# Due times of the first loads in a planned attention and convolution kernel: values of batch 0 one pair later, shared keys of batch 1 cast as they land

## The chip, the cores and the metric

The kernel runs on one core of a Trainium2 chip. The metric is the device time of one execution in microseconds (us). The span of a profile is the time from the first to the last instruction of one profiled execution.

The engines are named as the profile names them: PE is TensorE's matmul (PEld its weight load), DVE is VectorE, ACT is ScalarE, POOL is GpSimd, SP is SyncE, which here only issues DMAs.

## The reference

The input is q, k and v of 8 batches, 12 heads, 448 positions and 64 features, all float32, with three weight arrays. Attention has a softmax whose denominator has one more term; its result goes through a gated long convolution:

```python
scores = scale * np.matmul(q, k.transpose(0, 1, 3, 2))
m = np.max(scores, axis=-1, keepdims=True)
e = np.exp(scores - m)
attn = e / (np.sum(e, axis=-1, keepdims=True) + np.exp(-m) + 1e-09)
attn_out = np.matmul(attn, v)
...
proj = x @ w_proj                      # x: attn_out with the heads side by side, 448 x 768
x1, x2, x3 = three thirds of proj
X2 = np.fft.rfft(x2, n=S, axis=1)
H = np.fft.rfft(filter_fft, n=S, axis=0)
x2_conv = np.fft.irfft(X2 * H, n=S, axis=1)
y = x1 * x2_conv * x3
out = y @ w_out
```

## The kernel before, in words

**Work.** Heads are taken in pairs, six to a batch, so there are 48 pairs, numbered g = 0 to 47 through all batches. For a pair, TensorE makes scores transposed (keys on partitions; L662, L664), ScalarE takes the exponential (L670, L675), TensorE multiplies by the values with a column of ones beside them (L707, L712), and VectorE divides (L725 to L727). Then the result is turned so that features lie on partitions (`xT`). When the six pairs of a batch are done, the dense part of the batch follows: VectorE folds `xT` into sums and differences (`xf`, L819 to L827), TensorE projects the folded input with the middle third of the weights (L850, the first matmul of the dense part of batch 0), goes to the spectrum and back with small tables (L877, L962), makes the two gates (L923) and the output projection (L1035). Attention of the next batch runs between the pieces of the dense part.

**Keys in four blocks.** A head has 448 keys: three blocks of 128 and a rest of 64. The rests of the two heads of a pair share one block. So each batch has, for all six pairs, one load of the rest keys and one of the rest values into the buffer `rests` (L333). There is one such buffer for all batches, and one buffer `ks`, into whose diagonal halves the rest keys are cast (L372). Transposes of every pair of a batch read `ks`, so the cast of batch 1 comes after the transposes of pair 5, the last of batch 0. The rest values are cast into `vr` (L377), which exists twice.

**The first two batches.** Batches 0 and 1 are loaded as float32 by SyncE in `staged` (k and v: L321, 192 KB for a pair each; q: L316, two loads of 112 KB; the very first q comes by ScalarE's queue). They land in four staging slots, so pair g needs slot g mod 4, freed by the casts of pair g-4. GpSimd casts them to bf16 (k L343, q L349, v L356); TensorE turns k and q (L384, L386, L390). Batches 2 to 7 are cast by GpSimd's DMAs while they load (`loaded`). GpSimd also issues the loads of the weights (L640: three loads of 1152 KB, the middle third first; L645 for the output weights) and of the filter (L555 to L559).

**What sets the order.** `Plan` writes out the order of every engine before the kernel runs. Each piece of work is a task with an engine, an estimated length, a due time ("want"), the tokens that it needs, those that it makes, and the buffers that it takes and gives. Whenever an engine is free in the plan, it gets the ready task with the smallest due time. The chip executes the resulting order of each engine as it stands; the waits are semaphores put in by the framework. Due times in `staged` come from `tau(g)`: 6 + 3.5 g for the pairs of batch 0, 31 + 5.5 (g - 6) for those of batch 1. Loads are due `early` before that: 8 for batch 0, 14 for batch 1, with 0.1 between the three loads of a pair (k, q, v for batch 0; v, q, k for batch 1). The casts are due at tau(g) - 5 for k and q, and for v at tau(g) + 1 in batch 0 and tau(g) - 4 in batch 1. Each task can name tokens made when it starts (`begun`), such as `iv` 5 for the value load of pair 5; the weights' issues use them as gates (`GATES`): the middle third (part 1) is due at 12 and is ready once the value load of pair 5, the shared loads and the k and q loads of pair 7 have been issued in the plan.

Of the kernel before, what the change touches and what calls it, by code (L numbers as in the profile page):

```python
# [20 lines left out]
SP = 112  # L21
# [20 lines left out]
class Plan:  # L42
# [15 lines left out]
        self.size = rings  # L58
        self.tasks = []

    def add(self, eng, cost, want, emit, need=(), make=(), take=(), give=(), dma=0.0, run=256, n=1, after=0.0, begun=()):
        self.tasks.append((want, len(self.tasks), eng, cost, emit, need, make, take, give, dma, after, run, n, begun))

    def run(self):
        left = {}
# [16 lines left out]
        clock = 0.0  # L82
        landed = []

        def done(t, end, by):
            for k in t[6]:
                made[k] -= 1
                when[k] = (max(end, when.get(k, (0.0, by))[0]), by)
                heapq.heappush(events, end + self.LAT[by])
                heapq.heappush(events, end)  # L90
            for tok in t[8]:
                left[tok] -= 1
                if left[tok] == 0:
                    gone[tok] = end + self.LAT[by]
                    heapq.heappush(events, gone[tok])

        def transfers(to):
            nonlocal clock
            while clock < to:
                heads = {e: q[0] for e, q in queues.items() if q and q[0][0] <= clock + 1e-9}  # L100
                soon = [q[0][0] for q in queues.values() if q and q[0][0] > clock + 1e-9]
                if not heads:
                    clock = min([to] + soon)
                    continue
                total = sum(h[2][11] for h in heads.values())
                step = min([h[1] * total / h[2][11] for h in heads.values()] + [x - clock for x in soon] + [to - clock])
                clock += step
                for e, h in heads.items():
                    h[1] -= step * h[2][11] / total
                    if h[1] <= 1e-9:  # L110
                        queues[e].pop(0)
                        if e == "SP":
                            landed.extend([clock + self.LANDING] * h[2][12])
                        done(h[2], clock + self.LANDING, "SP")

        def ready(t):
            e = t[2]
# [23 lines left out]
        while any(queue.values()):  # L141
            moved = False
            for e in queue:
# [18 lines left out]
                if t[9]:  # L162
                    q = queues["POOL" if e == "POOL" else "SP"]
# [20 lines left out]
def kernel(  # L184
# [13 lines left out]
    MAGIC = 12582912.0  # L198
    NSTAGED = 2
    SPIN = 40  # L200
    EARLY1 = 14.0
    SLOT1 = 5.5
    BASE2 = 77.0
# [4 lines left out]
    RE1 = 4.0  # L208
    FT = 8.0
    GATES = (  # L210
        (1, [("iv", 5), ("ir", 1), ("ik", 7), ("iq", 7)]), ("F", [("cv", 8)]), (0, [("cv", 9)]), (2, [("cv", 10)]),
        ("O", [("cv", 11)]),
    )
    STEP = 1.5
    FOLD0 = (28.5, 29.0, 29.5)
# [60 lines left out]
    add = plan.add  # L276
    ATT0, SLOT0 = 6.0, 3.5
# [3 lines left out]
    def tau(i, frac=0.0):  # L281

        if i < NHP:
            return ATT0 + SLOT0 * (i + frac)
        if i < 2 * NHP:
            return BASE + SLOT1 * (i + frac - NHP)
        return BASE2 + (i + frac - 2 * NHP) * PERIOD / NHP
# [12 lines left out]
    def staged(b):  # L300
# [3 lines left out]
        for hp in range(NHP):  # L304
            g = b * NHP + hp
            want = tau(g) - early
            parts = (("k", k, 0, 384), ("q", q, 768, 512), ("v", v, 384, 384))
            if b:
                parts = parts[::-1]
            for n, (name, x, at, size) in enumerate(parts):  # L310
                src = stage(g, at, size)

                def load(name=name, x=x, src=src, hp=hp, g=g):
                    if name == "q":
                        for u in range(2):
                            (nc.sync if g else nc.scalar).dma_start(  # L316
                                src[0:SP, 256 * u : 256 * u + 256].rearrange("p (j d) -> p j d", j=NST),
                                q[b, 2 * hp + u].rearrange("(j p) d -> p j d", j=NST),
                            )
                    else:  # L320
                        nc.sync.dma_start(  # L321
                            src.rearrange("p (u c) -> p u c", u=2), rows(x, b, hp)
                        )

                need = [("c" + name, g - 4)] if g >= 4 else []
                old = g - 2 * NHP
                first = name == "q" and g == 0
                add("ACT" if first else "SP", 1.04 if name == "q" else 0.52, -21.0 if first else want + 0.1 * n, load, need=need,
                    make=[("s" + name, g)], dma=0.97 if name == "q" else 0.64, run=256 if name == "q" else 768,
                    n=2 if name == "q" else 1, begun=[("i" + name, g)])  # L330
                if hp == 0 and name != "q":
                    add("SP", 0.5, want + (0.05 if name == "k" else SLOT0 + 0.05) if b == 0 else want - RE1 + 0.1 * n,
                        lambda name=name, x=x: nc.sync.dma_start(rests[:, "kv".index(name)], shared(x, b)),  # L333
                        need=[("cr" + name, b - 1)] if b else (), make=[("r" + name, b)],
                        dma=0.75, begun=[("ir", b)])

                on_pool = name == "k" or g > 0
                eng = nc.gpsimd if on_pool else nc.vector

                def cast(name=name, src=src, hp=hp, g=g, eng=eng):  # L340
                    if name == "k":
                        T[g]["kn"] = t = ld.tile([128, 3, 128], BF16, name="k0")
                        eng.tensor_copy(  # L343
                            t[:].rearrange("p j (u d) -> p u j d", u=2),
                            src.rearrange("p (u j d) -> p u j d", u=2, j=3),
                        )
                    elif name == "q":
                        T[g]["qn"] = t = ld.tile([SP, NST, 2, DH], BF16, name="q0")
                        eng.tensor_copy(  # L349
                            t[:].rearrange("p j u d -> p u j d"),  # L350
                            src[0:SP].rearrange("p (u j d) -> p u j d", u=2, j=NST),
                        )
                    else:
                        sv = src.rearrange("p (u j d) -> p u j d", u=2, j=3)
                        for u in range(2):
                            nc.gpsimd.tensor_copy(  # L356
                                vn[b % 2][:, hp, 4 * u : 4 * u + 3, 0:DH], sv[:, u]
                            )

                T.setdefault(g, {})  # L360
                if name == "v":
                    add("POOL", 0.72, tau(g) + (1.0 if b == 0 else -4.0), cast,
                        need=[("sv", g)] + ([("V", old, 1)] if b >= 2 else []), make=[("cv", g), ("v", g)])
                else:
                    add("POOL" if on_pool else "DVE", 0.65 if on_pool else 0.42, tau(g) - 5.0, cast,
                        need=[("s" + name, g)] + ([("c" + name, g - 1)] if g else []), make=[("c" + name, g)], take=[(name + "0", g)])
            if hp == 0:
                for u in range(2):
                    c = slice(64 * u, 64 * u + 64)
                    on_pool = b > 0 or u == 1  # L370
                    add("POOL" if on_pool else "DVE", 0.55 if on_pool else 0.37, tau(g) - 5.9 if g else 3.0,
                        lambda c=c, on_pool=on_pool: (nc.gpsimd if on_pool else nc.vector).tensor_copy(  # L372
                            ks[c, :, c], rests[c, 0]
                        ),
                        need=[("rk", b), "zero ks"] + ([("T", NHP * b - 1)] if b else []), make=[("crk", b)])
                    add("POOL", 0.56, tau(g) + 1.0,
                        lambda c=c, u=u: nc.gpsimd.tensor_copy(vr[b % 2][c, :, u, 0:DH], rests[c, 1]),  # L377
                        need=[("rv", b), ("ones", b % 2)] + ([("V", NHP * (b - 1) - 1, 1)] if b >= 2 else []), make=[("crv", b), ("vr", b)])
# [41 lines left out]
            if g == 0:  # L420
# [5 lines left out]
                take=[hy], give=[("k0", g), ("q0", g)])  # L426
# [670 lines left out]
    with (  # L1097
# [39 lines left out]
        for i in range(2):  # L1137
            add("POOL", 0.7, (6.0, 24.0)[i], lambda i=i: ones(i), need=[("zero vr", i)], make=[("ones", i)],
                after=(6.5, 16.0)[i])
        for b in range(n_batches):  # L1140
# [5 lines left out]
            need=[("c" + x, g) for x in "kqv" for g in range(NHP * NSTAGED - NHP, NHP * NSTAGED)], make=["zero kn"])  # L1146
        for n, (part, key) in enumerate(GATES):
            load, size = {
                "F": (filter_load, 4.1), "O": (wout_load, 6.9),
            }.get(part, (lambda part=part: wproj_load(part), 6.9))  # L1150
            add("POOL", 1.6 if part == "F" else 0.95, 12.0 + 3 * n, load,
                need=[*key] + (["ft", "bps"] if part == "F" else []),
# [39 lines left out]
```

The softmax here doesn't subtract the row's maximum and nothing guards it: scores larger than these inputs give would overflow.

## Time and profile before

| measure | before |
|---|---|
| time, median of 3 runs (lowest to highest) | 389.67 us (388.77 to 391.54) |
| span of the profiled execution | 386.9 us |
| PE busy | 369.1 us, 95% |
| DVE busy | 268.7 us, 69% |
| ACT busy | 264.3 us, 68% |
| POOL busy | 113.5 us, 29% |
| mean DMA rate over the span | 130 GB/s |

The busy shares are averages over stages that differ. TensorE's first 4.3 us of work (1.84 to 6.15) are matmuls whose results nobody reads, before the first keys and queries are there (L1113). Attention of batch 0 follows, fed by SyncE's loads, then the dense parts, in which TensorE is almost never idle, and a tail in which only the last batch's dense part is left. GpSimd works mostly in the first third of the span: its casts serve the first two batches.

### The profile page before, as it was taken

The numbers are of one execution on the slowest core, as the hardware profiler recorded it, in microseconds if no ns is written. First come the engines' busy times: TensorE is split into PE (matmuls) and PEld (weight loads), VectorE is DVE, ScalarE is ACT, GpSimd is POOL, SyncE is SP. The second block draws the span as 40 slices with busy tenths as digits, with TensorE's granted clock in tenths as the row PEclk, the third lists the DMA queues.
The fourth block names the chain that finished last, engine by engine and source line by source line (L and its number), as shares of the span: only waits on it lengthen the run. The fifth ranks groups of instructions, "written<-read, shape, count | busy, mean of one in ns | idle before, by whom it ended". The sixth has DMA issues, their size and how long they took to land.

```text
span 386.9 us, 8977 instructions
## 1 busy us (share of the span) xinstructions
PE 369.1 (95%) x3461; PEld 232.1 (60%) x3461; DVE 268.7 (69%) x817; ACT 264.3 (68%) x460; POOL 113.5 (29%) x179
## 2 busy tenths in 40 slices
PE   6767999999999999999999999999999999999995
PEld 5444766656665566556655566556755666567652
DVE  6677669872888459956698439956699439964870
ACT  5778676737876758766876768766776758743543
POOL 7765818236340713332406222332100000000000
PEclk9999999999999999999999999999999999999998
DMA  9999999999999999799989699699941321012004
GB/s 203 239 247 234 208 208 177 147 134 214 139 150 112 224 164 128 99 115 163 138 127 87 145 153 162 81 109 156 123 70 26 126 56 29 15 54 84 0 2 164
DMA packets 179419, 50.44 MB, mean 130 GB/s; under 512 B 166125, under 2 KB 175792, under 8 KB 179376
## 3 DMA queue, kind: packets, MB, share of 16 engines
q0 software_dynamic: 101680, 17.80, 64.0%
q1 hardware_dynamic: 76768, 31.83, 41.9%
q8 instruction: 27, 0.44, 0.5%
q10 hardware_dynamic: 928, 0.23, 0.3%
q14 instruction: 16, 0.13, 0.1%
HBM read 43.86 MB, written 11.01 MB: 142 GB/s over the span
## 4 chain that ended last, share of the span: by engine, by line
PE 83%; DVE 6%; DMA 5%; ACT 3%; issue 2%; POOL 1%; SPq 0%; POOLq 0%; ACTq 0%
PE pps L923 24%; PE pps L850 16%; PE ops L1035 13%; PE op L712 8%; PE sc L662 7%; DMA wproj_bf<-in_moe_w_proj_dram 3%; PE op L707 3%; PE xsp L877 3%; PE cps L962 2%; PE sc L664 2%; PE sc L923 1%; DMA nat<-in_k_dram 1%; PE spin L1113 1%; PE sc L850 1%; DVE cv L991 1%
## 5 line engine op out<-in xcount | busy, mean ns | idle before, releaser
L670 ACT ACTIVATE e<-sc 128x896 bf16<-128x896 f32 x144 | 127.5, 922 | 16.3 <-PE sc L662 15.2
L923 PE MATMUL pps<-xT,wproj_bf 128*128 128x448 bf16 x522 | 110.6, 352 | 0.1
L923 PEld LDWEIGHTS <-wproj_bf 128*128 128x128 bf16 x576 | 52.0, 97 | 45.8 <-issue 5.9
L850 PE MATMUL pps<-wproj_bf,xf 128*113 128x384 bf16 x360 | 66.7, 328 | 1.0 <-DMA wproj_bf<-in_moe_w_proj_dram 0.8
L850 PEld LDWEIGHTS <-xf 128*113 128x113 bf16 x384 | 48.6, 132 | 16.4 <-issue 5.5
L712 PE MATMUL op<-vn,e 128*128 128x65 bf16 x1152 | 56.7, 194 | 0.0
L712 PEld LDWEIGHTS <-e 128*128 128x128 bf16 x1152 | 50.3, 97 | 5.2
L1035 PE MATMUL ops<-wout_bf,yT 128*128 128x384 bf16 x270 | 49.2, 326 | 0.1
L449 POOL DMA_DIRECT2D nat<-in_k_dram x36 | 29.8, 845 | 49.1 <-DMA kT<-nat 46.1
L727 DVE TENSOR_TENSOR xb<-op,rec 128x256 bf16<-128x256 f32 x96 | 40.7, 424 | 3.3
L725 DVE TENSOR_SCALAR rec<-op 128x4 f32<-128x4 f32 x96 | 15.2, 158 | 39.6 <-PE op L712 38.5
L707 PE MATMUL op<-vr,er 128*128 128x130 bf16 x192 | 42.1, 219 | 0.5 <-DVE xb L727 0.5
L662 PE MATMUL sc<-qT,kT 64*128 64x448 bf16 x288 | 40.5, 354 | 0.8 <-DVE qT L410 0.7
L1047 ACT COPY osb<-ops 128x384 f32<-128x384 f32 x52 | 24.2, 484 | 22.9 <-PE ops L1035 22.6
L1035 PEld LDWEIGHTS <-yT 128*128 128x128 bf16 x288 | 26.5, 98 | 20.0 <-DVE yT L1006 2.5
L891 DVE TENSOR_TENSOR t<-xs,hrs 113x768 bf16<-113x768 bf16 (+1 forms) x64 | 34.2, 552 | 5.8 <-ACT xs L885 5.6
L675 ACT ACTIVATE er<-sc 128x448 bf16<-128x448 f32 x48 | 26.6, 555 | 14.6 <-PE sc L664 14.0
L862 DVE CAST x<-pps 113x384 bf16<-113x384 f32 x32 | 17.7, 555 | 25.7 <-PE pps L850 25.6
L938 DVE TENSOR_TENSOR g<-x,pps 128x448 bf16<-128x448 bf16 x45 | 27.7, 616 | 6.9 <-PE pps L923 6.6
L971 ACT CAST cr<-cps 128x452 bf16<-128x452 f32 x48 | 26.0, 549 | 9.4 <-PE cps L962 9.2
L935 ACT CAST x<-pps 128x448 bf16<-128x448 f32 x42 | 22.9, 546 | 13.6 <-PE pps L923 12.6
L885 ACT CAST xs<-xsp 113x384 bf16<-113x384 f32 (+1 forms) x60 | 26.6, 492 | 3.8 <-PE xsp L877 3.2
(117 smaller groups left out, 462.1 us busy)
## 6 DMA issues: line engine op xcount, KB each, us to landing
out_dram<-osb SPq DMA_DIRECT2D x24, 384.0 KB, 2.4
nat<-in_q_dram POOLq DMA_DIRECT2D x24, 168.0 KB, 6.6
vn<-in_v_dram POOLq DMA_DIRECT2D x6, 672.0 KB, 10.9
wproj_bf<-in_moe_w_proj_dram POOLq DMA_DIRECT2D x3, 1152.0 KB, 12.2
nat<-in_k_dram POOLq DMA_DIRECT2D x36, 96.0 KB, 3.8
nat<-in_q_dram SPq DMA_DIRECT2D x22, 112.0 KB, 5.1
nat<-in_k_dram SPq DMA_DIRECT2D x12, 192.0 KB, 4.6
nat<-in_v_dram SPq DMA_DIRECT2D x12, 192.0 KB, 4.5
```

The lines of the kernel that those rows point to most:

```text
L449: nc.gpsimd.dma_start(kn[:, :, 1 + t, c], kr[:, :, 4 * u + t, :])
L662: nc.tensor.matmul(sc[:, u, 0:S], kT[b % 2][c, hp, t, :], qT[b % 2][c, hp, :])
L670: nc.scalar.activation(e[:, 0 : 2 * S].rearrange("p (u n) -> p u n", u=2), sc[:, :, 0:S], AF.Exp, scale=SCALE)
L675: nc.scalar.activation(e[:, 0:S], sc[:, 0, 0:S], AF.Exp, scale=SCALE)
L707: nc.tensor.matmul(op[:, n, :, :], e[0][:, o : o + 128], vr[b % 2][:, hp, :, :], start=True, stop=False)
L712: nc.tensor.matmul(op[:, n, u, :], e[1 + t][:, u * S + o : u * S + o + 128], vn[b % 2][:, hp, 4 * u + t, :], start=False, stop=(u == 1 and ...
L727: nc.vector.tensor_tensor(W["xb", b][:, hp, 2 * hf : 2 * hf + 2, :].rearrange("p t (u d) -> p t u d", u=2), op[:, :, :, 0:DH], rec[:].unsq ...
L850: nc.tensor.matmul(pps[:FQ, :DCH], W["xf", b][:, pg, kt, 0:FQ], wproj_bf[:, kt, D + ch * DCH : D + (ch + 1) * DCH], start=(kt == 0), stop= ...
L891: nc.vector.tensor_tensor(t[:K], L["xs", par, ch][:K], h, op=ALU.mult)
L923: nc.tensor.matmul(p[:, :S], wproj_bf[:, kt, 2 * part * D + dt * 128 : 2 * part * D + (dt + 1) * 128], xT()[:, kt, 0:S], start=(kt == 0), ...
L938: nc.vector.tensor_tensor(g[:, dt, :], L["x1", dt], p[:, :S], op=ALU.mult)
L1035: nc.tensor.matmul(ops[:n, :DCH], y[:, dt, 0:n], wout_bf[:, dt, ch * DCH : (ch + 1) * DCH], start=(dt == 0), stop=(dt == NDT - 1),)
```

## The change

Two due times are moved, with a third that follows from the first. The value loads of batch 0 are due 3.5 later, the distance of two pairs, so that a pair's values come behind the next pair's keys and queries: scores need keys and queries first and values only after the exponential. The load of the rest values of batch 0 is due 0.4 later, so that it stays behind the first value load. The cast of the rest keys of batch 1 is due 12 before its pair, where it was 5.9, so that it is preferred over other casts as soon as it is ready. A new field `late` of a task is used nowhere with a value, `REV` stands at the value that keeps the order as it was, and the line of `GATES` is only set differently.

```diff
@@ class Plan
-    def add(self, eng, cost, want, emit, ..., after=0.0, begun=()):
-        self.tasks.append((want, len(self.tasks), eng, ..., begun))
+    def add(self, eng, cost, want, emit, ..., after=0.0, begun=(), late=0.0):
+        self.tasks.append((want, len(self.tasks), eng, ..., begun, late))
...
-                        done(h[2], clock + self.LANDING, "SP")
+                        done(h[2], clock + self.LANDING + h[2][14], "SP")
...
+    VLATE = 3.5
+    CRK = 12.0
+    REV = True
...
@@ staged
-            if b:
+            if b and REV:
                 parts = parts[::-1]
...
-                add("ACT" if first else "SP", 1.04 if name == "q" else 0.52, -21.0 if first else want + 0.1 * n, load, need=need,
+                add("ACT" if first else "SP", 1.04 if name == "q" else 0.52, -21.0 if first else want + 0.1 * n + (VLATE if name == "v" and b == 0 else 0.0), load, need=need,
...
-                    add("SP", 0.5, want + (0.05 if name == "k" else SLOT0 + 0.05) if b == 0 else want - RE1 + 0.1 * n,
+                    add("SP", 0.5, want + (0.05 if name == "k" else SLOT0 + 0.45) if b == 0 else want - RE1 + 0.1 * n,
...
-                    add("POOL" if on_pool else "DVE", 0.55 if on_pool else 0.37, tau(g) - 5.9 if g else 3.0,
+                    add("POOL" if on_pool else "DVE", 0.55 if on_pool else 0.37, tau(g) - CRK if g else 3.0,
```

More of the change, by code (lines that the diff above doesn't have):

```diff
@@ L59, in __init__, with add @@
         self.tasks = []
-    def add(self, eng, cost, want, emit, need=(), make=(), take=(), give=(), dma=0.0, run=256, n=1, after=0.0, begun=()):
-        self.tasks.append((want, len(self.tasks), eng, cost, emit, need, make, take, give, dma, after, run, n, begun))
+    def add(self, eng, cost, want, emit, need=(), make=(), take=(), give=(), dma=0.0, run=256, n=1, after=0.0, begun=(), late=0.0):
+        self.tasks.append((want, len(self.tasks), eng, cost, emit, need, make, take, give, dma, after, run, n, begun, late))
     def run(self):
@@ L210 @@
     GATES = (
-        (1, [("iv", 5), ("ir", 1), ("ik", 7), ("iq", 7)]), ("F", [("cv", 8)]), (0, [("cv", 9)]), (2, [("cv", 10)]),
-        ("O", [("cv", 11)]),
+        (1, [("iv", 5), ("ir", 1), ("ik", 7), ("iq", 7)]), ("F", [("cv", 8)]), (0, [("cv", 9)]), (2, [("cv", 10)]), ("O", [("cv", 11)]),
     )
```

## The prediction, made before the changed kernel was run

> **What bounds the kernel now.** I first cut the span at the moments where TensorE changes its manner, with the busy time of each engine by stretch. Columns: stretch, its length, busy time (and instructions) of PE, PEld, DVE, ACT, POOL, then granted clock, DMA share and GB/s.
>
> ```profile
> 6.00:24.80 18.80, 14.79 (x215) 9.37 (x212) 13.21 (x45) 14.75 (x22) 12.80 (x40) 1.00 1.09 250
> 24.80:36.60 11.80, 6.56 (x97) 4.38 (x98) 9.02 (x33) 9.00 (x15) 9.43 (x20) 1.00 1.15 234
> 36.60:81.00 44.40, 44.02 (x436) 28.66 (x435) 34.78 (x107) 29.90 (x54) 21.04 (x28) 1.00 1.78 182
> 81.00:330.00 249.00, 247.82 (x2290) 153.55 (x2289) 173.50 (x527) 179.66 (x313) 66.27 (x77) 1.00 1.15 124
> ```
>
> From 36.6 to 330 us TensorE is idle for 0.38 + 1.18 = 1.6 us in all, and its work is the same in both kernels. So what happens before 36.6 counts in two ways only: when the saturated stretch begins, and how much TensorE work is done before it. TensorE idles 4.0 us from 6 to 24.8 us and 5.2 us from 24.8 to 36.6. Everything that the diff moves belongs to these first 37 us.
>
> What starts the saturated stretch is in the chain of waits (start, length, what):
>
> ```profile
> 14.59 5.14 DMA nat<-in_k_dram
> 19.80 0.45 issue
> 20.24 0.46 POOL k L343
> 20.78 0.62 POOL q L349
> 21.40 0.59 POOL vn L356 x2
> 21.99 2.16 issue
> 24.16 12.41 DMA wproj_bf<-in_moe_w_proj_dram
> 36.62 1.14 PE pps L850 x6
> ```
>
> The key load of pair 5 lands at 19.73, GpSimd casts k, q and v of that pair, then its next instruction is the issue of the first third of the projection weights (L640). That load lands at 36.57 and the first dense matmul of batch 0 starts at 36.62. The reader should see that it is GpSimd's *order of instructions*, not a data dependence, that ties the weight load to the loads of pair 5.
>
> A second chain ends at the same moment. TensorE's timeline (start, length, line, tile, in brackets the idle time before it) and GpSimd's:
>
> ```profile
> 24.25 0.55 PE L662 MATMUL sc<-qT,kT 64*128 64x448 bf16 x4
> 27.21 0.23 PE L384 MATMUL tps<-ident_bf,ks 128*128 128x128 bf16 x1 [2.41 <-POOL ks L372]
> 27.78 0.34 PE L386 MATMUL tps<-ident_bf,k 128*128 128x128 bf16 x3 [0.34 <-POOL k L343]
> ```
>
> ```profile
> 24.16 1.06 POOL L640 DMA_DIRECT2D wproj_bf<-in_moe_w_proj_dram  x1 [2.18 <-DMA nat<-in_q_dram]
> 25.23 0.63 POOL L349 CAST q<-nat 112x512 bf16<-112x512 f32 x1
> 25.78 1.37 POOL L372 CAST ks<-rests 64x384 bf16<-64x384 f32 x2
> 27.22 0.50 POOL L343 CAST k<-nat 128x384 bf16<-128x384 f32 x1
> ```
>
> The transposes of pair 6 wait 2.41 us for the shared-key cast of batch 1 (L372) and 0.34 us for a k cast, and the scores of pair 5 stand behind them in TensorE's order. From pair 5 the chain runs on through its softmax and its fold; VectorE writes the last fold parts for that matmul from 36.48 on (L827). So two chains, weights and fold, reach the first dense matmul within about 0.2 us of each other, and removing one alone gains nothing.
>
> **What the Trainium skill says.** "DMA: Bandwidth & Descriptors", section "Queues, rings and completion order", says that a DMA engine takes turns between the queues which have work. The trace agrees: the 1152 KB of weights take 12.41 us to land, some 95 GB/s, while the core moves 234 GB/s, so SyncE's loads take the rest. "SBUF — State Buffer", section "SBUF: two separate sides", says that GpSimd can't write DMA descriptors while VectorE holds the shared port. The 2.18 us before L640 are covered by VectorE work almost end to end (21.84 to 24.33), while the filter's DMA issue at 31.61 came with no idle time. That fits, but it may also be something paid once by the first such DMA; the trace doesn't decide. I keep the 2.2 us as it is.
>
> **Part by part.** The planner gives each engine, whenever it is free, the ready task with the smallest due time ("want"); the chip then runs that order.
>
> *Values one pair later.* The loads of batch 0 had k, q, v of pair g at -2, -1.9, -1.8 + 3.5g. With 3.5 added, v of pair g is due just behind q of pair g+1. In front of k and q of pair 5 one value load less is queued: v4 now goes behind them, v0 to v3 stay ahead. One is 192 KB; at the 250 GB/s of this stretch that is 197 kB / 250 = 0.79 us. So k5 lands at about 18.95 instead of 19.73 and its cast starts 0.8 us earlier. Where the trace had issued a pair's v before the q of the same pair (pairs 3 and 4), two loads move out of the way, 1.6 us, which removes most of TensorE's waits for q casts (1.08, 0.63 and 0.73 us at 9.9, 15.1 and 18.6). I cost this gain at nothing by itself: the dense matmul waits for the weights, and TensorE merely waits there instead.
>
> The values' own lateness is hidden. v goes behind one more k and q (192 + 224 KB, 1.7 us). The casts of v0 to v5 ended at 7.2, 13.2, 15.7, 16.7, 19.1 and 22.0, and the products that read them began at 11.7, 15.9, 20.0, 23.2, 28.8 and 32.3: slack 2.7 to 10 us. The shared values (from 1.55 to 1.95) drop behind q1, 224 KB or 0.9 us; their cast at 10.40 to 11.46 stood just ahead of the products at 11.65, and GpSimd did other work before it, so 0 to 0.5 us, in a stretch that waits later anyway. v5 falls behind v6, q6 and k6 (608 KB, 2.5 us), against 10 us of slack.
>
> *GpSimd's order at the weight issue.* The issue is due at 12 and gated on the starts of v5, k7 and q7 and the shared loads. v5 (now due at 19.2) still starts before pair 7 (22.5), so the same bytes precede the gate. v5's cast (0.59) is replaced ahead of it by v4's: no change of length. With k5 0.8 us earlier the issue is at about 23.4 instead of 24.16 and the weights land at about 35.8.
>
> *Shared keys earlier.* Due 19.0 instead of 25.1, so ahead of the casts of v4 (21), v5 (24.5), q6 and k6 (26). But it also needs pair 5's transposes, which end at 22.15 in the trace, since one buffer serves both batches: a due time cannot make it run before that. Ahead of q6's cast instead of behind it, it frees nothing: pair 6's transposes need all three. The casts (1.37 us) stay behind the weight issue in my forecast, and pair 6 gets its transposes about 0.8 us earlier, like all around it. The fold then ends about 0.8 us earlier too.
>
> The extra planner field and the flag at True do nothing.
>
> Sum: both chains 0.8 us earlier, the same TensorE work ahead: 389.67 - 0.8 = **388.9 us**.
>
> **Rivals.**
> (a) *The key casts get in front of the weight issue.* If in the plan pair 5's transposes end before the gate opens, due 19 against 24.5 puts them between q5's cast and the gate. GpSimd then waits for the transposes (22.15 - 0.8 = 21.35), casts for 1.37 (22.7), waits 2.2 and issues at about 24.9: 0.75 us later than now. Pair 6 is then faster, but the weights bound: 390.4 us. For it: the new number aims at that; against: the gate's due time of 12 wins whenever it is open.
> (b) *More is freed.* If the 2.2 us before the weight issue shrink with the other order on VectorE, weights land at 36.57 - 0.8 - 2.2 = 33.6, and the fold, without the 2.4 us stall, is at 36.7 - 0.8 - 2.4 = 33.5. Then 3 us: 386.6 us. For it: both waits are idle time that no data needs; against: both must go together.
> (c) *The new order costs.* Every later decision of the planner shifts with the head. TensorE's order may put less attention work before the first dense matmul (a score and two products, 0.5 + 0.4 us, idled away), or a batch may start with a bank or buffer wait: the 1.6 us of idle time from 36.6 to 330 would double. About +1.7: 391.4 us.
>
> **How the numbers follow.** Forecast 0.42, (a) 0.24, (b) 0.20, (c) 0.14. The range takes in most of (b) and (a) and stops at (c): 386.5 to 391.3. A change of 1% is 3.9 us; only (b) with more work pulled ahead, or (c) at several times its size, reaches that: faster 0.09, same 0.85, slower 0.06.
>
> **What would show it.** Right: k5's cast starts near 19.4, L640 near 23.4, first L850 near 35.8; q casts at pairs 1, 3 and 4 wait less; saturated stretch unchanged in idle time. The shared-key step is wrong if L372 stands before L640 on GpSimd. The forecast is wrong if the first L850 moves by more than 1.5 us, or if idle time from there to 330 us differs from 1.6 us by more than 1 us.

## The result and the profile after

| | before | after |
|---|---|---|
| time, median (lowest to highest, 4 runs each) | 389.92 us (388.77 to 391.54) | 394.21 us (393.15 to 395.12) |
| span of the profiled execution | 386.9 us | 393.3 us |
| PE busy | 369.1 us | 371.6 us |
| VectorE, ScalarE, GpSimd busy | 268.7, 264.3, 113.5 us | 270.8, 265.0, 113.6 us |

The ratio is 1.0106, with a 95% interval from 1.0061 to 1.0151. The change costs about 4.3 us. The forecast was a gain of 0.8 us, and 394.21 lies above the whole range. The two profiled executions lie further apart than the medians, 6.4 us in span: the one of after was the slowest of its four, and the one of before, at 388.65 us, was faster than the four in the table. Lines of the kernel after stand two further down than before: L642 is the weights' issue that was L640, L852 the dense matmul that was L850. Times and ratios in the table of experiments further down leave out disturbed, slower executions (five of 22 in e6, one each in e3, e9 and e11), and e11 has no profile there because its profile fell on one.

The windows view of the kernel after, with the stretches and columns of the prediction's first fence (stretch, length, busy time and instructions of PE, PEld, DVE, ACT, POOL, granted clock, DMA share, GB/s):

```profile
6.00:24.80 18.80, 14.41 (x177) 9.02 (x174) 11.20 (x38) 13.30 (x19) 12.70 (x42) 0.91 1.09 245
24.80:36.60 11.80, 8.06 (x124) 5.21 (x124) 11.18 (x35) 9.11 (x16) 10.78 (x21) 1.00 1.16 229
36.60:81.00 44.40, 42.42 (x421) 27.41 (x422) 34.91 (x104) 31.48 (x56) 21.30 (x29) 1.00 1.45 175
81.00:330.00 249.00, 244.42 (x2258) 150.94 (x2257) 169.07 (x516) 175.09 (x305) 64.82 (x75) 1.00 1.23 125
```

Take busy PE from the length of each stretch. Idle time from 6 to 36.6 us fell from 9.25 to 8.13 us. From 36.6 to 81 us it rose from 0.38 to 1.98 us, and from 81 to 330 us from 1.18 to 4.58 us. So the head, at which the change aims, idles less than before, and most of the loss lies where the forecast had placed none: 1.6 us of idle time have become 6.6 us. The rest of the difference between the two spans is busy time, 2.5 us more on TensorE; the granted clock of 0.91 in the first stretch belongs to it (see the last section).

**Where the order broke.** SyncE's timeline, first of the kernel before, then of the kernel after (start, length, line, load):

```profile
14.59 2.27 SPq L321 DMA_DIRECT2D nat<-in_k_dram  x1
16.90 0.99 SPq L316 DMA_DIRECT2D nat<-in_q_dram  x2
```

```profile
14.38 2.56 SPq L323 DMA_DIRECT2D nat<-in_k_dram  x1
16.98 0.47 SPq L323 DMA_DIRECT2D nat<-in_v_dram  x1
17.55 0.41 SPq L323 DMA_DIRECT2D nat<-in_k_dram  x1
18.06 0.42 SPq L323 DMA_DIRECT2D nat<-in_v_dram  x1
18.57 0.42 SPq L323 DMA_DIRECT2D nat<-in_k_dram  x1
19.09 0.42 SPq L323 DMA_DIRECT2D nat<-in_v_dram  x1
19.56 0.99 SPq L318 DMA_DIRECT2D nat<-in_q_dram  x2
```

The loads at 14.59 and 14.38 are k of pair 5. In the kernel before, q of pair 5 follows right behind it, at 16.90. In the kernel after five loads go in between, in the planned order v4, k6, v5, k7 and v6, all due later than q5 ("q5" is the query load of pair 5, and so on). The planner's code says why. SyncE may have at most nine loads open (`OPEN = 9`, test `out + t[12] > self.OPEN`), and a query load counts as two (`n=2`), since it is two DMAs, while keys and values count as one. When the planner comes to q5, eight of the nine slots are taken. It then gives the one free slot to the next ready load that fits, a single one, and does the same whenever one more slot comes free. A two-slot task is passed by one-slot tasks until two slots happen to be free together.

What it does to the head, in TensorE's timeline of the kernel before, then in TensorE's and GpSimd's of the kernel after:

```profile
21.79 0.36 PE L390 MATMUL tps<-ident_bf,q 112*128 112x112 bf16 x4
...
39.41 0.36 PE L390 MATMUL tps<-ident_bf,q 112*128 112x112 bf16 x4
```

```profile
26.15 0.37 PE L392 MATMUL tps<-ident_bf,q 112*128 112x112 bf16 x4 [0.40 <-POOL q L351]
...
38.44 2.24 PE L852 MATMUL pps<-wproj_bf,xf 128*113 128x384 bf16 x12
...
49.66 0.36 PE L392 MATMUL tps<-ident_bf,q 112*128 112x112 bf16 x4
```

```profile
26.62 1.07 POOL L642 DMA_DIRECT2D wproj_bf<-in_moe_w_proj_dram  x1
27.74 1.05 POOL L374 CAST ks<-rests 64x384 bf16<-64x384 f32 x2
...
34.37 0.88 POOL L642 DMA_DIRECT2D wproj_bf<-in_moe_w_proj_dram  x1
...
38.29 0.83 POOL L642 DMA_DIRECT2D wproj_bf<-in_moe_w_proj_dram  x1
43.45 0.89 POOL L351 CAST q<-nat 112x512 bf16<-112x512 f32 x1 [4.33 <-DMA nat<-in_q_dram]
```

The query transposes of pair 5 are at 26.15 where they were at 21.79. The weights' first issue is at 26.62 (24.16 before) and the first dense matmul at 38.44 (36.62). The other two thirds of the weights are issued earlier than before (34.37 and 38.29 against 40.28 and 45.25). The queries of pair 8 land so late that their cast waits 4.33 us and stands at 43.45, where it was at 33.97. Their transposes come at 49.66 us instead of 39.41, behind most of the first dense pieces of batch 0.

**Where the time is lost.** The two longest waits of TensorE from 36.6 to 330 us (engine, line, whom it waited for, us in all, times, longest); below it, the same view of SyncE's queue from 40 to 110 us:

```profile
PE pps L925 <- DVE g L940: 2.2, 2, 2.0
PE sc L666 <- DMA kT<-nat: 1.7, 1, 1.7
```

```profile
SPq L1056 <- ACT osb L1049: 9.9, 1, 9.9
```

The second line of the first view has a story. SyncE's timeline, first of the kernel before, then of the kernel after:

```profile
77.04 8.76 SPq L480 DMA_TRANSPOSE kT<-nat  x6
85.92 1.47 SPq L1054 DMA_DIRECT2D out_dram<-osb  x3
```

```profile
85.33 0.37 SPq L1056 DMA_DIRECT2D out_dram<-osb  x1
86.51 8.17 SPq L482 DMA_TRANSPOSE kT<-nat  x6
```

In the new order the first output store of batch 0 stands ahead of the six key transposes of batch 2. SyncE issues in order, so the transposes stand behind a store that waits 9.9 us for its data. They start 9.5 us later than before, and TensorE waits 1.7 us for the first keys of batch 2. The wait of 2.0 us for g is at 162 to 164 us, where VectorE stands for 2.70 us ahead of a copy within `xT`, with g two instructions behind it in its order:

```profile
162.98 0.17 DVE L821 COPY xT<-xT 128x6 bf16<-128x6 bf16 x1 [2.70 <-issue]
```

The profile names no releaser, but the DMA transpose into `xT` that SyncE issued at 155.97 took 6.9 us to land, until about 162.9. In the kernel before the same transpose, issued at 151.57, took 4.1 us, and VectorE did not stand there. So this wait, too, is a late DMA; what held it up was not isolated.

### The profile page after: what moved, and what is told of

It reads as the page before. It is cut to its first block, busy times and chain, and to the rows that moved or that the text cites. A ratio compares the mean times of both kernels' runs of the same rounds, so it can differ in the third digit from the quotient of the medians.

```text
span 393.3 us, 8987 instructions
## 1 busy us (share of the span) xinstructions
PE 371.6 (94%) x3461; PEld 232.7 (59%) x3461; DVE 270.8 (69%) x817; ACT 265.0 (67%) x460; POOL 113.6 (29%) x179
## 4 chain that ended last, share of the span: by engine, by line
PE 75%; DVE 10%; DMA 7%; SPq 3%; ACT 3%; issue 2%; POOL 0%; DVEq 0%; POOLq 0%; ACTq 0%
PE pps L925 22%; PE pps L852 13%; PE ops L1037 12%; PE op L714 7%; PE sc L664 7%; PE op L709 3%; DMA filt<-in_moe_filter_fft_dram 2%; PE cps L964 2%; PE sc L666 2%; PE xsp L879 2%; DMA kT<-nat 2%; DMA nat<-in_q_dram 1%; PE sc L925 1%; SPq L323 1%; DVE g L940 1%
## 5 line engine op out<-in xcount | busy, mean ns | idle before, releaser
L852 PE MATMUL pps<-wproj_bf,xf 128*113 128x384 bf16 x360 | 66.8, 328 | 0.7 <-DVE kT L402 0.7
L714 PE MATMUL op<-vn,e 128*128 128x65 bf16 x1152 | 57.7, 195 | 0.2 <-ACT e L672 0.2
L852 PEld LDWEIGHTS <-xf 128*113 128x113 bf16 x384 | 48.5, 132 | 15.5 <-issue 3.2
L714 PEld LDWEIGHTS <-e 128*128 128x128 bf16 x1152 | 51.2, 98 | 6.7 <-issue 0.8
```

The costliest lines, as they stand in the source:

```text
L714: nc.tensor.matmul(op[:, n, u, :], e[1 + t][:, u * S + o : u * S + o + 128], vn[b % 2][:, hp, 4 * u + t, :], start=False, stop=(u == 1 and ...
L852: nc.tensor.matmul(pps[:FQ, :DCH], W["xf", b][:, pg, kt, 0:FQ], wproj_bf[:, kt, D + ch * DCH : D + (ch + 1) * DCH], start=(kt == 0), stop= ...
```

## The experiments

Two theories at the start. **A**: the late query loads cost the time, because the planner lets single loads pass them. **B**: the later values themselves cost it, through casts and products that wait for them. The table has what the runs gave; "q5" and "q8" are the query transposes of pairs 5 and 8 on TensorE, "kT" the start of batch 2's key transposes, "idle" TensorE's idle time from 81 to 330 us in the profile. Each ratio compares with executions of the kernel before that were taken beside that kernel (medians of 389.6 to 390.1 us), so small differences between rows are better read from the ratios than from the times.

| kernel | time | ratio to before [95%] | q5 | q8 | kT | idle |
|---|---|---|---|---|---|---|
| before | 389.92 | | 21.79 | 39.41 | 77.04 | 1.18 |
| after | 394.21 | 1.0106 [1.0061, 1.0151] | 26.15 | 49.66 | 86.51 | 4.58 |
| e1 values late only | 395.97 | 1.0165 [1.0141, 1.0190] | 22.52 | 49.30 | 86.02 | 5.53 |
| e2 shared values only | 396.98 | 1.0182 [1.0153, 1.0212] | 24.19 | 49.29 | 86.70 | 5.29 |
| e3 after, queries as two tasks | 390.24 | 1.0022 [1.0002, 1.0042] | 21.69 | 41.33 | 75.43 | 1.21 |
| e4 before, queries as two tasks | 391.73 | 1.0039 [1.0021, 1.0057] | 22.55 | 42.84 | 76.73 | 1.53 |
| e5 after, store behind | 392.11 | 1.0048 [1.0019, 1.0077] | 25.14 | 48.80 | 82.54 | 3.00 |
| e6 before, store ahead | 391.29 | 1.0026 [0.9999, 1.0053] | 22.91 | 39.52 | 84.33 | 1.48 |
| e7 after, q5 one slot | 390.64 | 1.0028 [1.0010, 1.0045] | 22.61 | 39.12 | 75.92 | 1.25 |
| e8 e3, weights behind pair 6 | 390.14 | 1.0006 [0.9983, 1.0028] | 21.92 | 34.71 | 78.68 | 1.20 |
| e9 after, pairs 8 to 11 one slot | 400.11 | 1.0271 [1.0234, 1.0308] | 25.23 | 44.65 | 80.49 | 5.36 |
| e10 after, output weights early | 395.19 | 1.0137 [1.0093, 1.0182] | 25.27 | 48.53 | 89.12 | 3.13 |
| e11 e1, store behind | 394.35 | 1.0126 [1.0092, 1.0160] | | | | |
| e12 e1, q8 one slot | 391.98 | 1.0050 [1.0031, 1.0069] | 22.49 | 42.83 | 77.13 | 2.12 |

**e1 and e2: each half of the change alone.** Without the later shared keys, e1 keeps the later pair values and e2 only the later rest values.

```diff
 e1
-    CRK = 12.0
+    CRK = 5.9
-    ... SLOT0 + 0.45 ...
+    ... SLOT0 + 0.05 ...
 e2
-    VLATE = 3.5
-    CRK = 12.0
+    VLATE = 0.0
+    CRK = 5.9
```

> Only the value loads are due 3.5 later; shared values and shared keys have their old due times. In the planned order of loads q of pair 5 is then right behind k of pair 5, and only q of pair 6 comes late (behind k7, k8 and v7). Theory A (queries starved: a query load takes two of the planner's nine open slots, so single loads that are due later slip past it) expects most of the loss gone: transposes of pair 5 near 22 us instead of 26.2, time 390 to 392. Theory B (the late values themselves hold up what reads them, or the transfers) expects the changed kernel's time, 393 to 395.

> Only the load of the shared values of batch 0 is due 0.4 later, everything else as before. In the planned order q of pair 5 then starts behind v5, k6, k7 and v6, although no value of a pair is due later. Theory A (starved queries) expects the slow time without late values: transposes of pair 5 later than 25 us, time 393 to 395. Theory B (late values) expects the time of before, 389 to 391.

Either half alone costs more than the whole change by the medians (the intervals of e1 and after overlap). e2 speaks against B: no pair value is later in it, only one shared load has its due time moved by 0.4, and it loses as much as e1. Theory A missed its number in both: e2 lies above its 393 to 395, and in e1 q5 is in place (22.52), yet the kernel is slow all the same. So the place of q5 is a sign, not the whole cause. With the due time of the shared keys alone the planner writes the same order on all five engines as before, so that part is inert by itself.

**e3 and e4: no load needs two slots.** The two DMAs of a query load become two tasks of one slot each, in the kernel after (e3) and in the kernel before (e4).

```diff
-                add(..., 1.04 if name == "q" else 0.52, ..., load, need=need,
-                    make=[("s" + name, g)], dma=0.97 if name == "q" else 0.64, ...,
-                    n=2 if name == "q" else 1, begun=[("i" + name, g)])
+                for u in range(2 if name == "q" else 1):
+                    add(..., 0.52, ..., lambda u=u, load=load: load(u), need=need,
+                        make=[("s" + name, g)], dma=0.485 if name == "q" else 0.64, ...,
+                        begun=[("i" + name, g)])
```

> The changed kernel, with the two halves of each query load planned as two tasks of one slot each, so that they can't be passed for lack of a second slot. In the planned order q of pair 5 then follows k of pair 5 at once. Values are as late as in the changed kernel. Theory A (starved queries) expects 388 to 390.5, with the transposes of pair 5 near 21 us and the first dense matmul near 36. Theory B (late values) expects 393 to 395.

> The kernel before, with the same split of the query loads: the control for the third run. Its queries were not starved, so theory A expects about the time of before, 389 to 391; the difference to the third run is what the later values are worth when the queries keep their place, 0 to 1 us in their favour. Theory B expects the time of before too, and 3 to 5 us less than the third run.

With the values as late as in the change, e3 is about 0.2% from before; idle time from 81 to 330 us is back at 1.21 us. That settles B: late values do not cost the loss, and A is right that the cause lies in the placing of the query loads. Between e3 and e4 only the due times differ: with the query loads in place, the changed due times look worth 0.7 us by the ratios and 1.5 us by the medians, with intervals that overlap. Neither kernel is faster than before.

**e5 and e6: the store and the key transposes.** Only the order on SyncE is edited, by moving one row of the finished order: in e5 the store goes behind the six transposes, in e6 (the kernel before) it goes ahead of them.

```diff
+        i = next(n for n, (_, t) in enumerate(order) if ("store", 0, 0) in t[6])
+        row = order.pop(i)
+        at = [n for n, (_, t) in enumerate(order) if ("turn", 2) in t[6] and any(x[0] == "kT" for x in t[6])]
+        order.insert(at[-1] + 1, row)        # e6: at[0]
```

> The changed kernel; on SyncE's queue alone, the first output store of batch 0 is moved from ahead of the six key transposes of batch 2 to behind them. No other instruction changes its place. Theory A (the late queries push, in the plan, batch 2's loads behind the first output store, and on the chip that store, waiting for the dense part, holds the key transposes up) expects the transposes to start near 77 us instead of 86.5, TensorE's 1.7 us wait for them and some of what follows gone: 391.5 to 393. Theory C (the loss is made before 60 us, and the wait at 91 us only moves idle time) expects 393.5 to 395.

> The kernel before; on SyncE's queue alone, the first output store of batch 0 is moved from behind the six key transposes of batch 2 to ahead of them. No other instruction changes its place. Theory A expects the transposes to start near 86 us instead of 77 and 1.5 to 3.5 us more: 391.5 to 393.5. Theory C expects the time of before, 389 to 390.5.

e5 gains 2.1 us, about half the loss, and the 1.7 us of TensorE's wait for keys are gone; the wait for g stays (2.3 us). In e6 the transposes start at 84.33, nearly as late as in the kernel after, and no wait for them appears on TensorE. Its ratio leaves a loss of 0 to 2 us, below or at the lower end of the 1.5 to 3.5 us that A expected, and not clearly different from none. So a store ahead of the transposes makes TensorE wait where its order has the scores of these keys next, as in the kernel after at 91.7 us; in the order of before it does not. This makes it likely that the store costs less there, but the two intervals do not separate it.

**e7 and e9: which queries.** In e7 only q of pair 5 counts as one slot; in e9 the queries of pairs 8 to 11 do.

```diff
-                    n=2 if name == "q" else 1, ...
+                    n=2 if name == "q" and g != 5 else 1, ...       # e7
+                    n=2 if name == "q" and not g >= 8 else 1, ...   # e9
```

> The changed kernel, where the planner counts the query load of pair 5, and of no other pair, as one open slot instead of two. In the planned order q of pair 5 is then right behind k of pair 5, q of pair 6 behind v4, and the key transposes of batch 2 are ahead of the first output store again. Values are as late as in the changed kernel. Theory A (starved queries, of which pair 5's is the first) expects nearly all of the loss gone, 389.5 to 391.5. If the late values or the later queries' places cost by themselves, 392 to 395.

> The changed kernel, where the planner counts the query loads of pairs 8 to 11 as one open slot; those of pairs 5 to 7 stay at two. In the planned order q of pair 5 stays starved as in the changed kernel, q of pair 6 and the first weights come still later, but the last value load is early, the output weights load early, and the key transposes of batch 2 are ahead of the first output store. Theory T (what costs is the tail of the staged loads and what it does to batch 2) expects TensorE's idle time from 81 to 330 us back near 1.2 us and 391 to 393, with the first dense matmul later than in the changed kernel. Theory H (what costs is the late query of pair 5 at the head) expects 394 or more.

The weights' issue and the first dense matmul of e7:

```profile
24.23 1.06 POOL L642 DMA_DIRECT2D wproj_bf<-in_moe_w_proj_dram  x1 [1.23 <-issue]
```

```profile
36.31 2.16 PE L852 MATMUL pps<-wproj_bf,xf 128*113 128x384 bf16 x12 [1.05 <-DMA wproj_bf<-in_moe_w_proj_dram]
```

One number in one task takes most of the loss away (e7: 3.6 of 4.3 us by the medians, 1.06% to 0.28% by the ratios), although the planner then orders the later loads anew as well. And e9 is the slowest of all: q8 now passes q6 and q7, and q9 passes q7. The transposes of pair 5 stay late (25.23), and those of pairs 6 and 7 come at 31.56 and 41.95 us, where the kernel after had 29.52 and 36.96. Its last value load and its output weights are early, and its idle time is still 5.36 us, so the rival that only the late tail of the loads costs falls with it. The other side had said 394 or more and gave no upper bound. A part of this loss may be the clock's: it was 0.88 from 36.6 to 81 us in e9's profile, 1.00 in those of before and after.

**e10, e8 and e11: three further edits.** e10 issues the output weights right behind the last third of the projection weights, since their issue had moved from 46.66 to 58.37 us. e8 is e3 with the weights' first issue also gated on the casts of pair 6. e11 is e1 with the store behind, as in e5.

```diff
+        i = next(n for n, (_, t) in enumerate(order) if "wout" in t[6])      # e10
+        row = order.pop(i)
+        at = next(n for n, (_, t) in enumerate(order) if ("w", 2) in t[6])
+        order.insert(at + 1, row)
-        (1, [("iv", 5), ("ir", 1), ("ik", 7), ("iq", 7)]), ...                # e8
+        (1, [("iv", 5), ("ir", 1), ("ik", 7), ("iq", 7), ("ck", 6), ("cq", 6), ("crk", 1)]), ...
```

> The changed kernel; on GpSimd's order alone, the load of the output weights is moved from behind the last value cast (issued at 58.4 us) to right behind the last third of the projection weights (39 us). No other instruction changes its place. If this load beside batch 2's loads is what made their transposes late, the query transposes start near 65 us instead of 68.5 and the time falls by 0.5 to 1.5, to 392.5 to 393.7. If it then merely holds up the last staged loads instead, no change or slower, 394 to 395.5.

> The third run's kernel (changed, query loads in two tasks), with the issue of the middle third of the weights gated also on the casts of k and q of pair 6 and of the shared keys of batch 1. In the third run TensorE stood 2.9 us for the shared-key cast, which came behind the weight issue and the 2.6 us of idle time before it, and the clock was at half from about 24 us on. Theory A expects the transposes of pair 6 near 26 us instead of 28.5, no such stall, weights landing later than now but about with the fold: 388 to 390.5. If the weights are what bounds, 391 to 393.

> The first run's kernel (values late only, 396.0 us), with the first output store moved behind the six key transposes of batch 2 on SyncE's queue alone. Theory A expects the same gain as in the changed kernel, 1.5 to 2.5 us: 393.5 to 394.5, with the wait of 2.1 us for the key transposes gone. If the gain there was chance, 395.5 to 396.5.

e10 gains nothing, and batch 2's query transposes stay at 68.23 us (68.53 in the kernel after, 64.29 before): the late output weights are not what delays them. In e8 pair 6 no longer waits for its casts, but the first dense matmul waits 2.63 us for the weights; it ties with before and beats nothing. e11 gains 1.6 us over e1 by the medians and lies in the first of its expectations, though the intervals of the two ratios overlap a little.

**e12: pair 8.** What after, e1, e2, e5 and e10 share in the table are late transposes of pair 8 (48.5 to 49.7 us) and an idle time of 3.0 us or more; the kernels near before have q8 by 43 us. e1 and e7 have the transposes of pairs 5, 6 and 7 within 0.6 us of each other (22.52, 27.46, 34.38 against 22.61, 27.98, 34.90) and part at pair 8. e12 is e1 with the query load of pair 8 counted as one slot.

```diff
-                    n=2 if name == "q" else 1, ...
+                    n=2 if name == "q" and g not in (8,) else 1, ...
```

> The kernel is the one of the later pair values alone (395.97 us, ratio 1.0165), with the query load of pair 8 counted as one slot, so that it is issued ahead of the query loads of pairs 6 and 7. In the written order the transposes of pair 5 stay, those of pair 6 come later than in that kernel (by some 3 to 4 us), those of pair 7 stay, and those of pair 8 stand among the first dense pieces of batch 0 again, where they came at 49.3 us. Theory P: what the slow kernels share is that the transposes of pair 8 slip behind the first dense pieces (48.5 to 51.3 us where the kernels near the time of before have 39 to 43), and with them the amount of attention that is done by the time batch 2 begins; the time then comes back to 390.0 to 392.0 us, pair 8's transposes to under 43 us and the idle time of TensorE from 81 to 330 us to under 2.5 us. Theory M: it is the late queries of the middle pairs (6 here) that cost; they are later still in this kernel, so the time stays at 395.5 to 398 us, with over 4 us idle from 81 to 330 us.

TensorE's timeline, e1 and then e12: query transposes of pairs 6 and 8 each.

```profile
27.46 0.37 PE L392 MATMUL tps<-ident_bf,q 112*128 112x112 bf16 x4 [0.33 <-POOL q L351]
...
49.30 0.36 PE L392 MATMUL tps<-ident_bf,q 112*128 112x112 bf16 x4
```

```profile
31.43 0.37 PE L392 MATMUL tps<-ident_bf,q 112*128 112x112 bf16 x4 [2.40 <-POOL q L351]
...
42.83 0.36 PE L392 MATMUL tps<-ident_bf,q 112*128 112x112 bf16 x4
```

Pair 6 has become 4.0 us later and TensorE waits 2.40 us for it. Yet the kernel is 4.0 us faster than e1, with pair 8 back among the first dense pieces. The rest of the schedule comes back with it, as the windows view of e1 and then of e12 (81 to 330 us) and SyncE's timeline of e12 show:

```profile
81.00:330.00 249.00, 243.47 (x2245) 150.30 (x2242) 169.09 (x512) 174.60 (x304) 64.06 (x75) 1.00 1.22 125
```

```profile
81.00:330.00 249.00, 246.88 (x2283) 152.89 (x2281) 173.23 (x525) 176.75 (x308) 66.40 (x77) 1.00 1.12 123
```

```profile
77.13 8.79 SPq L482 DMA_TRANSPOSE kT<-nat  x6
87.89 4.18 SPq L1056 DMA_DIRECT2D out_dram<-osb  x3
```

Idle time falls from 5.53 to 2.12 us, and the store stands behind the transposes again without being moved by hand. So most of the loss in e1 is not from a late pair 6, which is later still in e12; it hangs on how the planner places the query load of pair 8. How much of the 4.0 us is the late pair itself, falling where TensorE has no idle time to give, and how much the orders that come back with it, the run does not separate: e11 moved the store alone for 1.6 of them.

**What stays open.** The slot count of q8 alone was changed only in e1, not in the kernel after, and e5 is as near to before as e12 with pair 8 still late (48.80). e9 has pair 8 at 44.65 and is the slowest; there pair 7 slips too, which no run takes apart. One rival stands untested. The filter and the other two thirds of the weights are gated on value casts (`cv` 8, 9 and 10 in `GATES`), and value loads pass query loads in the new orders, so these gates can open early. The second third of the weights goes out at 35.65 us in e1 and at 41.70 us in e12. Over all kernels it is issued at 32.1 to 36.0 us in after, e1, e2, e5, e9, e10 and e11, and at 38.9 to 44.9 us in before and in e3, e4, e6, e7, e8 and e12. This parts the slow kernels from those near before as well as pair 8 does. The early weights may be what makes the queries of pair 8 land late; no run held them back with the queries left as they were. Nor was it shown why e1 and e2 are slower than the whole change.

## Why the prediction was wrong

**The step that failed** is "Values one pair later", in its sentence "In front of k and q of pair 5 one value load less is queued". It took the due times as the order. The part on k5 came true: it is issued at 14.38 (14.59 before), and its cast starts at 19.54, where 19.4 was forecast and 20.24 was the time before. q5 was to come right behind it, with the weights' issue at 23.4; it came behind v4, k6, v5, k7 and v6, at 19.56, and the issue at 26.62. The limit on open loads and the two slots of a query load stand in the code that the prediction reads its due times from, and the prediction weighed only these times. e7 is the direct proof: with one slot for q5, and the values as late as in the change, the issue is at 24.23, the first dense matmul at 36.31 and the ratio 1.0028. It shows a second thing. With q5 in place the issue is still not at 23.4: GpSimd has two more casts ahead of it, half of the rest values of batch 1 and q of pair 6 (21.94 to 23.00). Neither e7 nor e3 (1.0022) is faster than before. So with the loads in the order that the forecast had assumed for k5 and q5, its gain of 0.8 us still did not appear.

**The premise that failed with it** is "Everything that the diff moves belongs to these first 37 us". The forecast had named its own test: idle time from there to 330 us within 1 us of 1.6 us, and the first dense matmul moved by no more than 1.5 us. Measured were 6.6 us and +1.82 us. The loads of batch 1 are due in the same stretch and share the limit, so the shift runs on to pair 8 and into every later order. e12 shows the weight of it: 4.0 us for the slot count of one query load, with all that the planner then orders otherwise.

**The values' lateness is hidden**: nearly right. The first product waits 0.72 us for the rest values (0 to 0.5 us were allowed), and the list of TensorE's waits has none for a pair value. Here is that wait in TensorE's timeline of the kernel after:

```profile
11.29 0.22 PE L709 MATMUL op<-vr,er 128*128 128x130 bf16 x1 [0.72 <-POOL vr L379]
```

**The gain at the first pairs**: right in kind. TensorE's waits for the query casts of pairs 1 and 3 fell from 1.08 to 0.29 and from 0.63 to 0.17 us; at pair 4 the wait grew from 0.73 to 2.02 us. With all query loads in place (e3 against e4) the changed due times look worth 0.7 to 1.5 us, but only against e4, which is itself slower than before.

**The shared keys earlier**: right, they change nothing by themselves. Their cast stays behind the weights' issue (27.74 behind 26.62), and rival (a) did not come about.

**Rival (c)**, that every later decision of the planner shifts, named what happened. Its size was wrong: idle time was to double, for +1.7 us; it quadrupled. The range stopped at this estimate, although nothing in the reasoning bounded it.

**The stall ahead of the weights, and the late pair 8.** The prediction kept the 2.18 us ahead of the weights' issue and held a lock by VectorE possible, as the Trainium skill describes it ("SBUF — State Buffer", section "SBUF: two separate sides"). In the kernel after GpSimd starts that issue without any wait at 26.62, while VectorE works with hardly a gap from 24.06 to 28.39 us. Over the kernels run, the stall was between 0 and 2.57 us. So in these runs it is neither a fixed price of the first such DMA nor set by VectorE's busy time alone; its cause stays open. What the Trainium skill says of turns between queues ("DMA: Bandwidth & Descriptors", section "Queues, rings and completion order") fits the queries of pair 8: their cast waits until 43.45 us for loads issued among those of 28.79 to 34.56 us, while weight loads of 1152 KB, issued from 26.62 us on, are under way and take 11.5 to 18.1 us to land.

## What to carry to other kernels

Where an order is computed from due times under a limit of open slots, a task that needs two slots can be passed by every later task that needs one; read the computed order, not the due times, before costing a change of them. A small shift near the start must be followed into the first stretch in which the busiest engine has no idle time: in this case a later pair 6 in the head did not cost what a later pair 8, past its beginning, seems to have cost. On an in-order DMA queue a store that waits for its data holds up every transfer behind it; what that costs depends on whether another engine needs those transfers by then.

## What was not expected of the hardware

**The granted clock of TensorE dips in some executions.** In the kernel after it was 0.91 on average from 6 to 24.8 us, against 1.00 before. The change need not be the reason. e6, whose instructions are in the order of before for the first 80 us, had 0.82 in that stretch, and e10, in the order of after until 38 us, had 1.00. e3 had 0.62 from 24.8 to 36.6 us. In these first stretches TensorE waits for loads anyway, and e6 and e3 have spans of 387.5 and 388.5 us all the same. Dips also fall later, where TensorE hardly idles: 0.88 in e9 and 0.93 in e12 from 36.6 to 81 us. There they lengthen busy time, which the idle times compared above do not show, and no run takes their share apart.
